# Splitting one group's output product around the next group's first layer in a fused attention and MLP kernel

## Chip, core and metric

The kernel runs on one core of one Trainium2 chip. The metric is device time in microseconds (us), the median of several runs. A core has five engines that work side by side, each through its own list of instructions in order: TensorE (PE: matmuls, with the weight loads in front of them), VectorE (DVE), ScalarE (ACT), GpSimd (POOL) and SyncE (SP, which here only issues DMAs). POOL and ACT issue some DMAs too. Matmul results go to PSUM, which the kernel treats as eight banks of 128 x 512 float32.

## What is computed

```
k_p, v_p = mean of k, v over 8 neighbouring positions       # q, k, v: (8, 8, 576, 64)
attn     = softmax(q @ k_p^T / sqrt(64)) @ v_p              # per batch and head
x        = attn as (4608 tokens, 512)
h        = x @ w_in                                         # w_in: (512, 2048)
out      = (h - tanh(h)) @ w_out                            # w_out: (2048, 512)
```

## The kernel before

**Groups.** The 4608 tokens are worked as nine groups of 512: groups 0 to 7 are the first 512 tokens of batches 0 to 7, group 8 is the eight remainders of 64. For each group there is a *first layer*: 16 tiles of 128 hidden rows x 512 tokens, four matmuls each, then a tanh on ACT and a subtract on DVE that writes g = h - tanh(h) as bf16 into `Gt`. Then comes the output product with w2 (`w_out`).

**Group 0** is special. Its first layer (lines 946 to 960) makes one tile at a time (`mlp_h`). Its output product is the plain one (`mlp_o`, line 586): four token blocks tb of 128, each a chain of 16 matmuls in one PSUM bank. The chains are done a quarter at a time in the order `W2_ORDER = (0, 8, 4, 12)`, so that a quarter of w2 (four of its sixteen row blocks) has to be there only when its turn comes. One *unit* below is four such matmuls, one tb and one quarter; there are 16. After a chain's last quarter ACT copies it to `O`, and after each second one SP stores two blocks.

**Groups 1 to 8** make the first layer in pairs (`h_pair`, line 616): tiles p and p + 8 into two neighbouring banks, one tanh and one subtract of 128 x 1024 for both. Pair 0 is computed in two halves of the tokens, since its second half needs the later x blocks. The eighth pair is made as two single tiles (`h_one`). The output product is done with seven products of half-size blocks instead of eight (`products`, line 689), for which DVE makes sums of `Gt` (`sum_p`, `sum_q`, `sum_d`) and the kernel once makes sums of w2's blocks b11, b12, b21, b22 (`w_sum`, line 647, into `w2s`; b12 itself is replaced by b22 - b12 at the end). Half of those sums is made on DVE, w2s 3 on POOL, and the negative of b22 (w2s 4) on ACT.

**Attention of the next batch** is laid between these. For batch 1 this falls into group 0's output product, in lines 961 to 1030, where the order is written out by hand by unit number u: POOL adds the raw keys together (`pool_k`, line 240; its last add, which makes `kd`, is DVE's here), ACT casts q to bf16 in three parts (`q1_cast` twice, then the last 64 tokens), PE turns keys and queries by matmuls with an identity (`k_transpose`, `q_pe_transpose`), DVE and ACT copy them out of PSUM (`KB`, `qT`), scores go through exp on ACT (`scores_wide`, `scores_ends`), DVE adds the values together and masks them into `VB` (`pool_v`, line 267), `av` (line 516) multiplies and DVE divides by the sums (a reciprocal and a multiply), and PE turns the five results of 128 tokens into xT (`x_pe_transpose`, copied by ACT), except the fifth, which belongs to group 8 and is turned by DMA. For the later batches queries, keys and x are turned by DMA transposes issued from SP, and `v_spread` places the values by three DMAs.

**PSUM banks** are given out by small counters: `Banks(5, 6, 7)` serves attention, banks 0, 1, 3, 4 hold the four output chains of group 0, and `h_pair` is told its first bank: (2, 0, 4, 6, 0, 2, 4) for group 1, (0, 2, 4, 6, 0, 2, 4) later.

**Queues.** Each engine follows the program's order; a tile framework adds the semaphores, and `after` adds a few waits by hand. w2 is loaded by POOL with a cast from float32 to float16: quarters 0 and 8 early (lines 812, 814), and inside `pool_k(1)` blocks 4 and 5, 6 and 7 after the first add and quarter 12 after the second (line 961, `mid`). SP's order through this part is: batch 1's queries and values (lines 943, 944), a transpose for group 8, batch 2's keys (line 963, held until blocks 6 and 7 of w2 have landed), values and queries, group 0's stores, then in group 1's loop the transposes of batch 2's keys and x end at pair 0, its queries at pairs 2, 3 and 4 (`c = p - 2`, each right behind ACT's cast `q_cast_part`), the three spreads, and batch 3's keys, values and queries. In group 1's products SP issues the transposes of batch 2's x, which group 2's first layer reads.

Of the kernel before, what the change touches and what calls it, by code (L numbers as in the profile page):

```python
# [20 lines left out]
R = 4  # L21
# [6 lines left out]
TG = 512  # L28
# [15 lines left out]
def kernel(  # L44
# [192 lines left out]
    def halves(n, b):  # L237
        return ((0, n),) if b < 2 else ((0, n // 2), (n // 2, n))

    def pool_k(b, eng, t0=0, t1=NT, mid=(), last=None, dep2=None):  # L240
        r = k_raw[b % 2].rearrange("p t (j d) -> p t j d", d=D)[:, t0:t1, :, :]
        if b not in kdups:
            kdups[b] = work.tile([128, NT, 2, D], BF16, name="kd", tag="kd", bufs=1)
        kd = kdups[b][:, t0:t1, :, :]
        n = t1 - t0
        for ta, tb in halves(n, b):
            eng.tensor_tensor(  # L247
                out=r[:, ta:tb, 0:4, :], in0=r[:, ta:tb, 0:4, :], in1=r[:, ta:tb, 4:8, :], op=ALU.add
            )
        for i, m in mid[0:2]:  # L250
            load_w2(i, m)
        second = eng.tensor_tensor(
            out=r[:, :, 0:2, :], in0=r[:, :, 0:2, :], in1=r[:, :, 2:4, :], op=ALU.add
        )
        if dep2 is not None:
            after([second], dep2)
        for i, m in mid[2:]:
            load_w2(i, m)
        kd_done = (last or eng).tensor_tensor(
            out=kd,  # L260
            in0=r[:, :, 0:1, :].to_broadcast([128, n, 2, D]),
            in1=r[:, :, 1:2, :].to_broadcast([128, n, 2, D]),
            op=ALU.add,
        )
        return kd_done

    def pool_v(b, eng):
        r = v_raw[b % 2].rearrange("p t (j d) -> p t j d", d=D)
        for ta, tb in halves(NT, b):
            eng.tensor_tensor(  # L270
                out=r[:, ta:tb, 0:4, :], in0=r[:, ta:tb, 0:4, :], in1=r[:, ta:tb, 4:8, :], op=ALU.add
            )
        eng.tensor_tensor(
            out=r[:, :, 0:2, :], in0=r[:, :, 0:2, :], in1=r[:, :, 2:4, :], op=ALU.add
        )
        if b < 2:
            eng.tensor_tensor(
                out=r[:, :, 0, :], in0=r[:, :, 0, :], in1=r[:, :, 1, :], op=ALU.add
            )
            v_main(VB[b % 2], r[:, :, 0:1, :], eng, 0, NM)  # L280
            return v_left(VB[b % 2], r[:, NM, 0:1, :], eng)
        if b < 4:
            eng.memset(VB[b % 2][0:G, 0:H, D:D1], float(POOL))
        vps[b] = work.tile([128, NT, D], BF16, name="vp", tag="vp", bufs=1)
        return eng.tensor_tensor(
            out=vps[b][:, :, :], in0=r[:, :, 0, :], in1=r[:, :, 1, :], op=ALU.add
        )

    vps = {}

# [5 lines left out]

    def v_main(vb, vs, eng, t0, t1):
        n = t1 - t0
        eng.tensor_tensor(
            out=vb[:, 2 * t0 : 2 * t1, 0:D].rearrange("p (t s) d -> p t s d", s=2),  # L300
            in0=vs[:, t0:t1, :, :].to_broadcast([128, n, 2, D]),
            in1=mask[:, 2 * t0 : 2 * t1, :]
            .rearrange("p (t s) o -> p t s o", s=2)
            .to_broadcast([128, n, 2, D]),
            op=ALU.mult,
        )
# [276 lines left out]

    o_tiles = {}

    def mlp_o(g, tb, qd, gts, pool=None, k0=0, k1=4):
        if qd == 0:
            p, tag = pool or (ps_o, "o_ps")
            o_tiles[tb] = p.tile([128, DM], FP32, name="o_ps", tag=tag)
        o_ps = o_tiles[tb]  # L590
        i0 = W2_ORDER[qd]
        for i in range(i0 + k0, i0 + k1):
            nc.tensor.matmul(  # L593
                o_ps[:, :],
                lhsT=gts[i][:, tb * 128 : (tb + 1) * 128],
                rhs=w2b[:, i, :],
                start=(i == 0),
                stop=(i == NHID - 1),
            )
        if qd == 3:  # L600
            nc.scalar.copy(out=O[:, tb, :], in_=o_ps[:, :])
            if tb % 2:
                store(g, tb - 1, tb + 1, nc.sync)
# [337 lines left out]
    ps_h.n = ps_o.n = 0  # L941
    nc.scalar.copy(out=q_bf[:QT, R, :, :], in_=t0[:QT, :, R, :])
    load_q(1, False)
    load_main(v_pairs, v_raw[1], 1, 0, NM)
    load_q_tail(1, q_raws[1], nc.scalar)
    for i in range(5):
        mlp_h_mms(0, i, 2, 4)
# [1 line left out]


    for i in range(5, NHID):
        mlp_h(0, i, gts, bank((0, 1, 2, 3, 4, 0, 1, 2, 3, 4, 2)[i - 5], [128, TG]))
        if i == 7:
            q_pe_tail(0)
        if i == 9:
            scores_tail(0)
        if i == 11:
            ps_a.n = 0
            av(0, 4, ps_any, True)
            x_dma_transpose(0, 2)  # L960
    kd1 = pool_k(1, nc.gpsimd, mid=((4, 2), (6, 2), (12, 4)), last=nc.vector)
    after([w_sum(w2s[:, 3, :, :], b21, b11, ALU.subtract, nc.gpsimd, k, k + 2) for k in (0, 2)], kd1)
    after(load_k(2), w2_dmas[3])
    load_v(2)

    def q1_cast(t, h):
        nc.scalar.copy(
            out=q_bf[:, 0:R, h : h + 4, :].rearrange("p j h d -> p h j d"),
            in_=t[:, h : h + 4, 0:R, :],
        )  # L970

    o_pools = [(ps_o, "o_ps"), (ps_o, "o_ps"), (ps_h, "hT_ps"), (ps_h, "hT_ps")]
    pend = []
    for u in range(16):
        qd, tb = u // 4, u % 4
        if u == 8:
            scores_wide(1, (3,))
            scores_ends(1)
        if qd == 2:
            for t2 in (2 * (tb % 2), 2 * (tb % 2) + 1):  # L980
                mlp_o(0, t2, qd, gts, o_pools[t2], tb // 2 * 2, tb // 2 * 2 + 2)
        else:
            mlp_o(0, tb, qd, gts, o_pools[tb])
        if u == 0:
            q1 = q_raws.pop(1)
            q1_cast(q1, 0)
        if u == 3:
            k_transpose(1, ps_any, (nc.vector.tensor_copy, nc.vector.tensor_copy))
        if u == 4:
            q_pe_transpose(1, (0, 1), "act")  # L990
            q1_cast(q1, 4)
            nc.scalar.copy(out=q_bf[:QT, R, :, :], in_=q1[:QT, :, R, :])
            load_q(2)
            w_sum(w2s[:, 1, :, :], b11, b12, ALU.add, k1=4)
            w_sum(w2s[:, 0, :, :], b11, b22, ALU.add, k1=4)
            w_sum(w2s[:, 2, :, :], b21, b22, ALU.add, k1=4)
            w_sum(b12, b22, b12, ALU.subtract, k1=4)
            v1_done = pool_v(1, nc.vector)
            after(
                [  # L1000
                    w_sum(w2s[:, 3, :, :], b21, b11, ALU.subtract, nc.gpsimd, k, k + 2)
                    for k in (4, 6)
                ],
                v1_done,
            )
            w_sum(w2s[:, 1, :, :], b11, b12, ALU.add, k0=4)
        if u in (5, 6):
            q_pe_transpose(1, (u - 3,), "act")
        if 5 <= u <= 7:
            scores_wide(1, (u - 5,))  # L1010
        if u == 6:
            q_pe_tail(1)
        if u in (9, 11):
            n = (u - 9) // 2
            nc.scalar.mul(
                out=w2s[:, 4, 4 * n : 4 * n + 4, :], in_=b22[:, 4 * n : 4 * n + 4, :], mul=-1.0
            )
        if 11 <= u <= 14:
            x_pe_transpose(1, *pend.pop(0))
        if 9 <= u <= 12:  # L1020
            pend.append((u - 9, av(1, u - 9, ps_any, False)))
        if u == 13:
            w_sum(w2s[:, 0, :, :], b11, b22, ALU.add, k0=4)
            sums = w_sum(w2s[:, 2, :, :], b21, b22, ALU.add, k0=4)
        if u == 15:
            ps_a.n = 0
            av(1, 4, ps_any, True)
    pool_k(2, nc.gpsimd, dep2=sums)
    pool_v(2, nc.gpsimd)
    w_sum(b12, b22, b12, ALU.subtract, k0=4)  # L1030

    for g in range(1, NG):
        nb = g + 1 if g + 1 < B else None
        nn = g + 2 if g + 2 < B else None
        for p in range(NP - 1):
            c = p if g > 1 else p - 2
            if nb is not None and 0 <= c < 3:
                q_cast_part(nb, c)
            h_pair(g, p, ((2, 0, 4, 6, 0, 2, 4) if g == 1 else (0, 2, 4, 6, 0, 2, 4))[p], p % 2)
            if 3 <= p < 6:  # L1040
                sum_p(2 * p - 6, 2 * p - 4)
            if nb is not None and p == 0:
                k_dma_transpose(nb)
            if g == 1 and p == 0:
                x_dma_transpose(1, 2)
            if g > 1 and p == 0:
                store(g - 1, 2, 4, nc.gpsimd)
                store(g - 1, 0, 2, nc.gpsimd)
            if nb is not None and p == 0:
                k_place(nb, nc.gpsimd.tensor_copy)  # L1050
            if nb is not None and 0 <= c < 3:
                q_dma_transpose(nb, c)
# [6 lines left out]
        h_one(g, NP - 1, 1, 0, 2)  # L1059
        h_one(g, NP - 1, 0, 1, 3)  # L1060
        sum_p(6, 8)
        sum_q(0, 4)
        sum_q(4, 8)
        if nb is not None:
            sum_d(0, 2)
            sum_d(2, 4)
        ps_a = Banks(2, 3, 4, 5, 0, 1)
        for u in range(14):
            n, half = u // 2, u % 2
            bk, lhs, rhs = products[n]  # L1070
# [57 lines left out]
```

The softmax here doesn't subtract the row's maximum and nothing guards it: scores larger than these inputs give would overflow.

## Time and profile before

| | us |
|---|---|
| median of three runs (lowest, highest) | 286.85 (286.12, 287.18) |
| the profiled execution | 289.25 |
| its span, first to last instruction | 287.5 |
| PE busy in it | 276.5 (96%) |
| DVE, ACT, POOL busy | 221.3, 158.0, 113.8 |
| granted TensorE clock | 1.00 |
| group 0's output product with batch 1's attention | 34.84 to 56.15 |
| group 1's first layer, its products | 56.15 to 71.64, 71.64 to 87.31 |
| group 2's first layer, its products | 87.31 to 101.30, 101.30 to 116.30 |

A line of the timeline reads: start in us from the span's start, length, engine, line of the kernel, operation, tile written <- tiles read, shapes, number of instructions merged, and in brackets the idle time of that engine just before, with what ended it. "PEld" is the weight load of PE, "SPq" a DMA issue on SP. A line of the chain of waits has start, length and what the chain went through. A line of the DMA issues has the tiles, the issuing queue, the number, the size of one in KB and the median us from issue to landing. A line of the table by stretch has the stretch, its length, the busy us of PE, PEld, DVE, ACT and POOL with the number of instructions, the granted clock, the DMA engines' share and GB/s.

### The profile page before, as it was taken

To read this page: it belongs to the slowest core of one execution; us is meant where nothing else is said; L and a number is where in the kernel's file an instruction comes from. 1 tells how busy PE (TensorE), PEld (TensorE's weight loads), DVE (VectorE), ACT (ScalarE), POOL (GpSimd) and SP (SyncE) were. 2 spreads that over 40 slices of the span, in tenths; PEclk is the share of its full clock that TensorE was granted. 3 is DMA by queue.
4 is the path that set the end of the run, shared out by engine and by line. 5 is a ranking of instruction groups with operands and counts; after the bars stand their busy time and mean duration, and the time that the engine had idled before them with its cause. 6 is when DMAs were issued, how large, how long until landed. Compare 5 with 4: busy or idle time off the path is not lost.

```text
span 287.5 us, 5465 instructions
## 1 busy us (share of the span) xinstructions
PE 276.5 (96%) x2156; PEld 179.7 (63%) x2156; DVE 221.3 (77%) x338; ACT 158.0 (55%) x212; POOL 113.8 (40%) x124
## 2 busy tenths in 40 slices
PE   7799989997999999999999999999999999999994
PEld 3364444643796479647964796479647964884583
DVE  6567878748985898589858985898589838945993
ACT  4637656757817681768176817681768146315510
POOL 8500650794089208920892089208930110000000
PEclk9999999999999999999999999999999999999999
DMA  7999999995997898689859965798560350002014
GB/s 242 229 213 264 308 123 187 328 275 107 295 233 113 222 339 202 85 215 350 191 102 222 355 160 100 227 335 177 101 186 0 51 179 0 2 40 109 0 36 112
DMA packets 67253, 50.41 MB, mean 175 GB/s; under 512 B 42652, under 2 KB 56476, under 8 KB 67228
## 3 DMA queue, kind: packets, MB, share of 16 engines
q1 hardware_dynamic: 57724, 36.04, 50.0%
q0 software_dynamic: 6784, 12.06, 19.9%
q10 hardware_dynamic: 2720, 1.97, 2.4%
q8 instruction: 17, 0.28, 0.4%
q14 instruction: 8, 0.07, 0.1%
HBM read 36.70 MB, written 9.44 MB: 160 GB/s over the span
## 4 chain that ended last, share of the span: by engine, by line
PE 84%; DMA 7%; DVE 3%; ACT 2%; issue 1%; SPq 1%; ACTq 0%
PE PS L665 34%; PE PS L608 34%; PE PS L564 5%; DMA q_raw<-in_q_dram 4%; PE PS L448 3%; PE PS L593 3%; DMA k_raw<-in_k_dram 3%; PE PS L422 3%; DVE Gt L622 2%; PE PS L374 1%; DVE P L630 1%; ACT TS L621 1%; PE PS L463 1%; ACT qT L132 0%; PE PS L844 0%
## 5 line engine op out<-in xcount | busy, mean ns | idle before, releaser
L608 PE MATMUL PS<-xT,w1b 128*128 128x512 bf16 (+1 forms) x504 | 98.1, 355 | 1.5 <-DVE Gt L622 1.5
L622 DVE TENSOR_TENSOR Gt<-PS,TS 128x1024 bf16<-128x1024 f32 x56 | 68.4, 1221 | 35.3 <-ACT TS L621 35.3
L608 PEld LDWEIGHTS <-w1b 128*128 128x128 f16 x576 | 56.3, 98 | 54.3 <-issue 1.8
L621 ACT ACTIVATE TS<-PS 128x1024 f32<-128x1024 f32 x56 | 57.3, 1024 | 29.3 <-PE PS L608 27.1
L709 POOL TENSOR_TENSOR m<-O,m 128x512 f32<-128x512 f32 x6 | 7.6, 1260 | 78.5 <-ACT m L707 78.5
L665 PE MATMUL PS<-w2s,Dg 128*128 128x256 f16 x256 | 30.2, 273 | 0.0
L247 POOL TENSOR_TENSOR k_raw<-k_raw 128x512 f32<-128x512 f32 (+2 forms) x13 | 21.4, 1665 | 18.7 <-DMA k_raw<-in_k_dram 18.7
L443 ACT ACTIVATE E<-PS 72x1024 bf16<-72x1024 f32 (+1 forms) x30 | 26.1, 930 | 4.2 <-PE PS L422 4.0
L665 PEld LDWEIGHTS <-Gt 128*128 128x128 bf16 x256 | 23.5, 98 | 6.8 <-issue 2.3
L665 PEld LDWEIGHTS <-P 128*128 128x128 bf16 x256 | 24.5, 98 | 3.0
L665 PEld LDWEIGHTS <-Dg 128*128 128x128 bf16 x256 | 24.6, 98 | 2.8
L630 DVE TENSOR_TENSOR P<-Gt 128x1024 bf16<-128x1024 bf16 x32 | 22.1, 689 | 0.6
L716 ACT COPY m<-PS 128x512 f32<-128x512 f32 x8 | 4.7, 586 | 29.5 <-PE PS L665 29.5
L640 DVE TENSOR_TENSOR Dg<-Gt 128x1024 bf16<-128x1024 bf16 x32 | 20.4, 683 | 0.0
L681 POOL DMA_DIRECT2D out_dram<-O x14 | 7.7, 552 | 31.7 <-DVE O L719 29.5
L270 POOL TENSOR_TENSOR v_raw<-v_raw 128x512 f32<-128x512 f32 (+1 forms) x12 | 18.2, 1535 | 0.0
L499 DVE TENSOR_TENSOR x_sb<-PS,rden 128x512 bf16<-128x512 f32 x24 | 16.6, 692 | 0.8
L665 PE MATMUL PS<-w2s,Gt 128*128 128x256 f16 x128 | 16.4, 273 | 0.0
L665 PE MATMUL PS<-w2b,P 128*128 128x256 f16 x128 | 16.3, 273 | 0.0
L665 PE MATMUL PS<-w2b,Gt 128*128 128x256 f16 x128 | 16.3, 272 | 0.0
L665 PE MATMUL PS<-w2s,Q 128*128 128x256 f16 x128 | 16.3, 272 | 0.0
L1090 ACT COPY O<-PS 128x512 f32<-128x512 f32 x7 | 4.1, 586 | 21.9 <-PE PS L665 21.9
(120 smaller groups left out, 401.8 us busy)
## 6 DMA issues: line engine op xcount, KB each, us to landing
k_raw<-in_k_dram SPq DMA_DIRECT2D x7, 1024.0 KB, 5.8
q_raw<-in_q_dram SPq DMA_DIRECT2D x7, 1024.0 KB, 10.7
v_raw<-in_v_dram SPq DMA_DIRECT2D x7, 1024.0 KB, 7.9
out_dram<-O POOLq DMA_DIRECT2D x14, 512.0 KB, 3.9
w1b<-in_moe_w_in_dram POOLq DMA_DIRECT2D x4, 512.0 KB, 15.6
w2b<-in_moe_w_out_dram POOLq DMA_DIRECT2D x3, 512.0 KB, 25.3
out_dram<-O SPq DMA_DIRECT2D x2, 512.0 KB, 9.1
k_raw<-in_k_dram SPq DMA_DIRECT2D x7, 128.0 KB, 5.9
```

What stands on the lines that cost most here:

```text
L247: eng.tensor_tensor(out=r[:, ta:tb, 0:4, :], in0=r[:, ta:tb, 0:4, :], in1=r[:, ta:tb, 4:8, :], op=ALU.add)
L270: eng.tensor_tensor(out=r[:, ta:tb, 0:4, :], in0=r[:, ta:tb, 0:4, :], in1=r[:, ta:tb, 4:8, :], op=ALU.add)
L422: nc.tensor.matmul(dst, lhsT=kv[a * D : (a + 1) * D, m, :], rhs=rhs, start=True, stop=True,)
L443: nc.scalar.activation(out=e, in_=ps, func=ACT.Exp, scale=SCALE)
L499: nc.vector.tensor_tensor(out=x_sb[:, :, :, :], in0=ps[:, :, :, 0:D], in1=rden[:, :, :, :].to_broadcast([128, 2, 4, D]), op=ALU.mult,)
L564: nc.tensor.matmul(h_tiles[i][:, :], lhsT=w1b[:, fb, i * 128 : (i + 1) * 128], rhs=xT[g][:, :, fb, :], start=(fb == 0), stop=(fb == NFB - 1),)
L608: nc.tensor.matmul(dst[:, t0 * 128 : t1 * 128], lhsT=w1b[:, fb, i * 128 : (i + 1) * 128], rhs=x[:, t0:t1, fb, :], start=(fb == 0), stop=(f ...
L621: nc.scalar.activation(out=t2, in_=PS[:, b0 : b0 + 2, :], func=ACT.Tanh)
L622: nc.vector.tensor_sub(out=Gt[:, p, :, :], in0=PS[:, b0 : b0 + 2, :], in1=t2)
L630: nc.vector.tensor_tensor(out=P[:, a:b, :], in0=Gt[:, a:b, 0, :], in1=Gt[:, a:b, 1, :], op=ALU.add)
L640: return nc.vector.tensor_tensor(out=Dg[:, a:b, :, :], in0=Gt[:, a:b, :, 0:HT], in1=Gt[:, a:b, :, HT:TG], op=ALU.subtract,)
L665: nc.tensor.matmul(part(g, bk, tt), lhsT=lhs(k, slice(tt * 128, (tt + 1) * 128)), rhs=rhs[:, k, :], start=(first and k == 0 and (tt == 0 o ...
```

## The change

Four things are moved, and the hand-written loop over u becomes a straight list.

1. Group 0's 16 units are no longer done in a row. Ten of them (quarters 0 and 8 of all four blocks, quarter 4 of blocks 0 and 1) stay among batch 1's attention; the other six are a function, `rest_of_group_0`, which is called in group 1's loop ahead of pair 4, with four of DVE's sums and the last b12 sum behind it. The chains use banks 1, 2, 3, 0, and group 1's pairs the banks (6, 4, 6, 4, 6, 4, 2).
2. POOL issues w2's last two quarters as two whole loads behind the key adds and two of its w2 sums, instead of three loads between the adds. Batch 2's key load waits for quarter 4, which is now one load.
3. Batch 1's values are loaded in two halves and pooled on DVE in three parts (`pool_v1`): the leftover rows early, each half later.
4. In group 1, batch 2's query casts and transposes, key transpose, spreads and batch 3's loads move from pairs 2, 3, 4 (the key transpose: 0) to pairs 4, 5, 6 (4).

All five AV blocks of batch 1 now use two neighbouring banks at once, and all three casts of q stand ahead of the query turns on ACT.

```diff
+    def pool_v1(ta, tb):
+        r = v_raw[1].rearrange("p t (j d) -> p t j d", d=D)
+        for n in (4, 2, 1):
+            nc.vector.tensor_tensor(
+                out=r[:, ta:tb, 0:n, :],
+                in0=r[:, ta:tb, 0:n, :],
+                in1=r[:, ta:tb, n : 2 * n, :],
+                op=ALU.add,
+            )
+        if ta == NM:
+            return v_left(VB[1], r[:, NM, 0:1, :], nc.vector)
+        return v_main(VB[1], r[:, :, 0:1, :], nc.vector, ta, tb)
...
-            o_tiles[tb] = p.tile([128, DM], FP32, name="o_ps", tag=tag)
+            o_tiles[tb] = bank((1, 2, 3, 0)[tb], [128, DM])
...
-    load_main(v_pairs, v_raw[1], 1, 0, NM)
+    load_main(v_pairs, v_raw[1], 1, 0, 2)
+    load_main(v_pairs, v_raw[1], 1, 2, 4)
...
-        mlp_h(0, i, gts, bank((0, 1, 2, 3, 4, 0, 1, 2, 3, 4, 2)[i - 5], [128, TG]))
+        mlp_h(0, i, gts, bank(i % 5, [128, TG]))
...
-    kd1 = pool_k(1, nc.gpsimd, mid=((4, 2), (6, 2), (12, 4)), last=nc.vector)
-    after([w_sum(w2s[:, 3, :, :], b21, b11, ALU.subtract, nc.gpsimd, k, k + 2) for k in (0, 2)], kd1)
-    after(load_k(2), w2_dmas[3])
-    load_v(2)
...
+    ps_a = Banks(4, 5, 6, 7)
+    q1 = q_raws.pop(1)
+    kd1 = pool_k(1, nc.gpsimd, last=nc.vector)
+    after([w_sum(w2s[:, 3, :, :], b21, b11, ALU.subtract, nc.gpsimd, k, k + 2) for k in (0, 2)], kd1)
+    load_w2(4, 4)
+    load_w2(12, 4)
+    w_sum(w2s[:, 1, :, :], b11, b12, ALU.add, k1=4)
+    pool_v1(NM, NT)
+    mlp_o(0, 0, 0, gts)
+    q1_cast(0)
+    q1_cast(4)
+    nc.scalar.copy(out=q_bf[:QT, R, :, :], in_=q1[:QT, :, R, :])
+    mlp_o(0, 1, 0, gts)
+    mlp_o(0, 2, 0, gts)
+    k_transpose(1, ps_any, (nc.vector.tensor_copy, nc.vector.tensor_copy))
+    w_sum(w2s[:, 0, :, :], b11, b22, ALU.add, k1=4)
+    w_sum(w2s[:, 2, :, :], b21, b22, ALU.add, k1=4)
+    mlp_o(0, 3, 0, gts)
+    q_pe_transpose(1, (0, 1), "act")
+    mlp_o(0, 0, 1, gts)
+    scores_wide(1, (0,))
+    q_pe_transpose(1, (2,), "act")
+    pool_v1(0, 2)
+    mlp_o(0, 1, 1, gts)
+    scores_wide(1, (1,))
+    q_pe_transpose(1, (3,), "act")
+    q_pe_tail(1)
+    w_sum(b12, b22, b12, ALU.subtract, k1=4)
+    v1_done = pool_v1(2, 4)
+    mlp_o(0, 2, 1, gts)
+    scores_wide(1, (2, 3))
+    scores_ends(1)
+    mlp_o(0, 3, 1, gts)
+    ps_a.n = 0
+    av(1, 0, ps_any, True)
+    av(1, 1, ps_any, True)
+    mlp_o(0, 0, 2, gts)
+    turn1(0)
+    turn1(1)
+    av(1, 2, ps_any, True)
+    mlp_o(0, 1, 2, gts)
+    av(1, 3, ps_any, True)
+    after(load_k(2), w2_dmas[2])
+    load_v(2)
+    load_q(2)
+    av(1, 4, ps_any, True)
+    turn1(2)
+    turn1(3)
...
+    for n in range(2):
+        nc.scalar.mul(out=w2s[:, 4, 4 * n : 4 * n + 4, :], in_=b22[:, 4 * n : 4 * n + 4, :], mul=-1.0)
+    after(
+        [w_sum(w2s[:, 3, :, :], b21, b11, ALU.subtract, nc.gpsimd, k, k + 2) for k in (4, 6)],
+        v1_done,
+    )
+    w_sum(w2s[:, 1, :, :], b11, b12, ALU.add, k0=4)
+    w_sum(w2s[:, 0, :, :], b11, b22, ALU.add, k0=4)
+    sums = w_sum(w2s[:, 2, :, :], b21, b22, ALU.add, k0=4)
+    x_dma_transpose(1, 2)
     pool_k(2, nc.gpsimd, dep2=sums)
     pool_v(2, nc.gpsimd)
-    w_sum(b12, b22, b12, ALU.subtract, k0=4)
+
+    def rest_of_group_0():
+        for qd, tb in ((2, 2), (2, 3), (3, 0), (3, 1), (3, 2), (3, 3)):
+            mlp_o(0, tb, qd, gts)
+        sum_p(2, 4)
+        sum_q(0, 4)
+        sum_d(0, 2)
+        sum_d(2, 4)
+        w_sum(b12, b22, b12, ALU.subtract, k0=4)
...
-            c = p if g > 1 else p - 2
+            c = p if g > 1 else p - 4
+            if g == 1 and p == 4:
+                rest_of_group_0()
             if nb is not None and 0 <= c < 3:
                 q_cast_part(nb, c)
-            h_pair(g, p, ((2, 0, 4, 6, 0, 2, 4) if g == 1 else (0, 2, 4, 6, 0, 2, 4))[p], p % 2)
+            h_pair(g, p, ((6, 4, 6, 4, 6, 4, 2) if g == 1 else (0, 2, 4, 6, 0, 2, 4))[p], p % 2)
...
-            if nb is not None and p == 0:
+            if nb is not None and c == 0:
                 k_dma_transpose(nb)
-            if g == 1 and p == 0:
-                x_dma_transpose(1, 2)
...
-        ps_a = Banks(2, 3, 4, 5, 0, 1)
+        ps_a = Banks(*((4, 5, 2, 3, 0, 1) if g == 1 else (2, 3, 4, 5, 0, 1)))
```

## Prediction

> **What bounds it now.** I read the busy table by stretch first, then the chain that ended last, then the timelines of PE, ACT, DVE and SP from 34 to 90 us. The clock is 1.00 in every stretch, so busy PE time can be compared. Stretches (columns: length, then busy us of PE, PEld, DVE, ACT, POOL):
>
> ```profile
> 56.15:71.64 15.49, 14.00 (x76) 7.03 (x74) 10.63 (x12) 9.71 (x11) 11.72 (x12) 1.00 0.92 203
> 71.64:87.31 15.67, 15.17 (x169) 12.77 (x168) 14.80 (x25) 7.14 (x10) 7.22 (x5) 1.00 1.06 261
> 87.31:101.30 13.99, 13.99 (x76) 7.19 (x74) 9.93 (x11) 10.52 (x12) 7.99 (x11) 1.00 0.73 161
> 101.30:116.30 15.00, 15.00 (x171) 12.68 (x169) 14.00 (x24) 6.59 (x9) 7.38 (x5) 1.00 0.88 253
> 34.84:56.15 21.31, 20.04 (x152) 10.65 (x151) 16.05 (x34) 14.33 (x25) 8.97 (x8) 1.00 1.24 216
> ```
>
> Group 2, rows three and four, is PE end to end: 13.99 us of first layer, 15.00 of products. The change sits in the others: group 0's output product with batch 1's attention (**O**, last row, 21.31), group 1's first layer (**H**, first row, 15.49) and its products (**P**, second row, 15.67). H and P are 1.50 and 0.67 longer than group 2's. In O, 64 output matmuls are 64/16 x 3.45 = 13.8 (sixteen ran from 34.84 to 38.29) and the attention's small ones about 5.85 (41 turns of 0.056, the query tail 0.1, scores 1.7, AV 30 x 0.059), so 1.6 to 1.7 is waiting. All that can be won here is about 3.8 us. The chain and the timelines say why H waits:
>
> ```profile
> 50.29 12.59 DMA q_raw<-in_q_dram
> ...
> 63.91 1.02 ACT TS L621
> ```
>
> ```profile
> 58.16 1.02 ACT L621 ACTIVATE TS<-PS 128x1024 f32<-128x1024 f32 x1 [1.57 <-PE PS L608]
> ...
> 59.21 1.23 DVE L622 TENSOR_TENSOR Gt<-PS,TS 128x1024 bf16<-128x1024 f32 x1 [0.59 <-ACT TS L621]
> ...
> 62.95 1.04 ACT L184 CAST q_bf<-q_raw 128x1024 bf16<-128x1024 f32 x1 [2.05 <-DMA q_raw<-in_q_dram]
> ...
> 69.91 1.89 PE L608 MATMUL PS<-xT,w1b 128*128 128x512 bf16 x8 [1.49 <-DVE Gt L622]
> ```
>
> ACT stands before batch 2's query cast until the load lands at 62.9; tanh, subtract and PE follow late. One pair costs PE 13.83/8 = 1.73, ACT 1.02, DVE 1.23. The last thing to see is SP's queue, whose chain ends just in time:
>
> ```profile
> 71.28 0.58 SPq L138 DMA_DIRECT2D k_raw<-in_k_dram  x1
> ...
> 81.68 4.12 SPq L527 DMA_TRANSPOSE xT<-x_sb  x2
> ```
>
> ```profile
> q_raw<-in_q_dram SPq DMA_DIRECT2D x1, 1024.0 KB, 11.9
> ```
>
> Batch 3's loads start at 71.28; its queries (issued 73.82) land 11.9 later, at 85.7, which is 14.4 after the first issue. Batch 2's two x transposes, issued behind them on the same queue, land at 86.95 and 87.86, though their inputs were ready before 84: they waited for the loads. Group 2's first layer starts at 87.31 and needs the second at 87.31 + 0.86. The slack is 0.3 us.
>
> **The change, in order of time (us of the profiled execution).**
>
> *Start of O.* POOL's second key add no longer stands behind two DMA issues: it ends at 34.14 + 1.56 = 35.7 instead of 37.1. DVE's last group-0 subtract ends at 36.36, so kd (0.82) ends at 37.2, 0.8 earlier. PE does three units (four matmuls, 0.864 each) to 37.43, turns the keys, one unit to 38.6, and waits as before for the query cast (38.34 + 1.04 = 39.4), whose load I leave where it was. ACT now makes all three casts first (38.34 to 40.9), so qT 0 is copied at 41.4, not 40.5. On DVE a w2 sum (1.13, as the first beside POOL's sum now) and the leftover values (0.43 + 0.29 + 0.22 + 0.42 with gaps 1.5) go ahead of the KB copies, which end at 40.9, not 39.7. The first scores start at 41.45; PE waits 0.7. From there ACT paces it: last exp at 46.5 (47.0 before).
>
> *Values in halves.* Per half: 0.70 + 0.43 + 0.29 + 0.44, 1.95 with gaps. DVE: KB 40.9, two w2 sums 42.3, half one 44.25, b12 sum 44.95, half two 46.9. The whole load had landed by 44.2 before, so DVE sets this. The first AV matmuls run at 46.6 to 46.9, a microsecond before the 47.91 of now. This edit gains 1.0.
>
> *AV and turns.* But only ten of sixteen units are left to fill PE here, and AV blocks follow each other through DVE: reciprocal and multiply take 0.94 a block, 0.6 after its matmuls. Ends of the multiplies: 48.3, 49.24, 51.1 (after turn 1), 52.3, 53.24. PE waits about 0.7 before turn 1 and 0.85 before turn 2, whose banks AV 3 holds. Group 1's first pair writes banks 6 and 7, which AV 4 holds: it starts at 53.3. Six units (5.18) are still owed then, so this is like 58.5 against 56.15 now.
>
> *w2's last quarters.* Their issues move behind POOL's add, kd and two POOL sums (2.26): to 39.6 and 40.3 from 34.1, 34.8 and 37.05. The rows they move away from:
>
> ```profile
> w2b<-in_moe_w_out_dram POOLq DMA_DIRECT2D x2, 256.0 KB, 11.8
> w2b<-in_moe_w_out_dram POOLq DMA_DIRECT2D x1, 512.0 KB, 13.1
> xT_last<-x_end SPq DMA_TRANSPOSE x1, 11.5
> ```
>
> Ends: the store row's 3.9 for 512 KB gives 43.5; 13.1 gives 52.7. The w2 packets that started around 38 each took about 5 us, beside the transpose that took 11.5 and lagging value packets. I take 12.3 less 5.2: landed at 46.7, needed by PE at 47.45; no cost. The upper end costs 5.2. The last quarter then lands near 50 to 52, before its users at 54.8 (ACT) and 63 (PE). Batch 2's loads hang on the third quarter, 47.1 before, so they don't move.
>
> The Trainium skill, "DMA: Bandwidth & Descriptors", Anatomy of one DMA, gives such a DMA 2.0 us plus bytes over 436 GB/s; for 1 MB read that is an estimate of 4.4 us, against rows of 11.3 to 13.1 here. By the page alone the quarter lands near 44.7, by the longest row at 52.7.
>
> *Four pairs on two pairs of banks.* The output tiles keep banks 0 to 3, so pairs 0 to 3 alternate between 6,7 and 4,5; pair 2 waits for pair 0's subtract. Also ahead of tanh 0 on ACT are the turns' copies (to 53.9) and two w2 negations (1.06 each, to 55.9). Pair 0 ends on PE at 55.1, its tanh at 56.9, subtract at 58.1; pair 2 starts at 58.2 where PE was free at 56.8. That wait of 1.4 comes once; pair 3 ends at 61.7. The six units then run to 66.8, ACT and DVE catch up in them, and pairs 4 to 7 end H at 73.75. Now: 71.64. **+2.1.** The wait for batch 2's queries is gone (their cast comes at 67.5, the load lands at 62.9): that is H's 1.50, already in this sum. DVE's sums that move ahead of P can give back up to P's 0.67.
>
> *SP's queue.* Query casts move from pairs 2, 3, 4 to pairs 4, 5, 6. ACT reaches the first only behind the fourth O copy (67.5); the others follow tanh 4 and 5, the last ending at 72.15 (67.28 now). Behind it on SP stand a transpose (1.2) and three spreads (2.7): batch 3's loads are issued at 76.2, 2.4 after H's end, where now it is 0.36 before. From first issue to queries landed the other groups show 12.6, 13.2, 13.0 and 14.0, this one 14.4; from there to the first x transpose 1.25. Taking 13.4 + 1.3: group 2 starts at 90.9. PE alone would get there at 73.75 + 15.0 to 15.67 = 88.8 to 89.4. So SP's queue ends last. 90.9 - 87.31 = **+3.6**; with 12.6 to 14.4, 2.8 to 4.6. From group 2 on the order is the old one, period 28.8, PE bound, so the shift stays to the end. POOL's keys and values of batch 2 were ready at 61.65 and 67.2 and are not late; the spread lands about 78, AV of batch 2 starts about 80.
>
> **Sum.** The profiled execution took 289.25 us with a span of 287.5; the median of the runs shown is 286.85, 2.4 below. I put the difference on the median: 286.85 + 3.6 = **290.5**.
>
> **Rivals.**
> 1. *Only PE's own waits count*: batch 3's loads run at DMA speed with no engine lagging, x is in time. For: 13 of the 16 DMA engines' shares of that query load had landed by 83.84, and the last came at 85.70. Against: four more groups take at least 12.6. Then 73.75 + 15.0 to 15.67: +1.5 to +2.1, 288.6.
> 2. *The third w2 quarter late*: PE stands at 47.45 until up to 52.7, and all behind it. For: the rows of 11.3 to 13.1. Against: the stuck packets. PE's order lets nothing pass the waiting matmul, so 2 to 5 us come on top of the forecast: 292.5 to 295.5.
> 3. *Faster*: the waits in O and H together cost only what O's cost now (1.65), since H's wait for the queries is gone. Its place is tanh 0 and pair 2's bank wait; H would end at 34.84 + 19.65 + 13.85 + 1.65 = 70.0, and with products of 15.0 group 2 starts at 85.0: -2.3, 284.5. It decides from the point where H ends before 70.9 and batch 3's loads go out before 71.2. Against: pair 2's wait is arithmetic, 1.02 + 1.23 against 1.73, and SP's casts are three pairs from the end.
> 4. *Nothing*: H's gain and O's loss cancel and the loads are just in time, or the split changes who waits only: 286.9.
>
> **Chances.** Forecast 0.50 (289.3 to 291.8); rival 1 0.17, of which 0.02 within 0.5%; rival 2 0.12; rival 3 0.08; rival 4 0.13. Slower by over 0.5% (1.4 us, about what a measurement of this kernel can tell from no change): 0.50 + 0.15 + 0.12 = 0.77; within: 0.15; faster: 0.08. The range leaves out rival 3 and most of rival 2: 286.6 to 292.8.
>
> **What would show it.** AV 0 before 47.2; group 1's first matmul near 53.3; PE waiting for a Gt subtract before pair 2, near 57 to 58; the six late units unbroken around 62 to 67; H's end near 73.7; batch 3's first load near 76; PE waiting for xT at group 2's start, near 89 to 91. I am wrong if the first layer of group 1 ends before 72, if the loads go out before 73, or if PE stands in front of w2b near 47.

## The result and the profile after

| | before | changed |
|---|---|---|
| median of four runs (lowest, highest), us | 286.49 (285.71, 287.18) | 294.49 (294.15, 297.21) |
| ratio, 95% interval | | 1.0297 [1.0239, 1.0355] |

The changed kernel is slower, as forecast, but by 8.0 us and not by 3.6. The stretches of its profiled execution (297.21 us, span 295.3) are, in the columns of the table by stretch: group 0's ten units with attention (O), group 1's first layer up to the six late units, those units, the rest of the layer (these three are H), the products (P), and group 2's first layer.

```profile
35.33:54.10 18.77, 15.04 (x129) 8.33 (x128) 16.39 (x33) 9.99 (x18) 7.86 (x8) 1.00 0.84 209
54.10:63.09 8.99, 7.24 (x41) 3.99 (x41) 7.09 (x6) 5.52 (x7) 7.62 (x6) 1.00 0.71 197
63.09:68.27 5.18, 5.18 (x25) 2.35 (x24) 4.68 (x5) 2.78 (x4) 4.30 (x4) 1.00 0.04 18
68.27:75.18 6.91, 6.91 (x34) 3.18 (x33) 5.59 (x8) 6.42 (x8) 0.97 (x3) 1.00 0.93 245
75.18:93.41 18.23, 14.98 (x168) 12.49 (x167) 12.64 (x21) 8.21 (x11) 10.63 (x7) 0.99 0.91 228
93.41:108.90 15.49, 15.49 (x74) 7.97 (x75) 9.45 (x10) 8.98 (x10) 4.52 (x9) 0.90 0.79 191
```

Length less the first busy number is PE's idle time: 3.73 in O, 1.75 in the first piece of H, none beside the late units or after them, 3.25 in P. Group 2's first layer has no idle time and is still 1.5 longer than the 13.99 of before: its granted clock is 0.90. The timeline of PE names the waits:

```profile
42.28 0.38 PE L377 MATMUL PS<-qT,KB 128*128 128x512 bf16 x1 [1.74 <-DVE KB L325]
...
59.48 3.61 PE L610 MATMUL PS<-xT,w1b 128*128 128x512 bf16 x16 [1.75 <-DVE Gt L624]
...
93.41 0.82 PE L610 MATMUL PS<-xT,w1b 128*128 128x256 bf16 x3 [3.25 <-DMA xT<-x_sb]
```

The chain of waits goes through the same places: DVE's three w2 sums and a subtract ahead of pair 2, then PE, then the DMA transpose of x.

```profile
54.04 4.25 DVE w2s L650 x3
58.29 1.14 DVE Gt L624
59.48 3.61 PE PS L610 x16
63.09 5.18 PE PS L595 x24
68.27 6.91 PE PS L610 x32
...
84.37 8.99 DMA xT<-x_sb
93.41 15.49 PE PS L610 x72
```

Batch 2's query cast no longer waits for its load, but it comes late, between the last O copy and tanh 4 (ACT), and SP's queue follows it: batch 3's first load is issued at 77.58 (71.28 before), and x waits in the queue behind these loads.

```profile
68.79 1.05 ACT L184 CAST q_bf<-q_raw 128x1024 bf16<-128x1024 f32 x1
```

```profile
77.58 0.58 SPq L138 DMA_DIRECT2D k_raw<-in_k_dram  x1
...
84.37 7.16 SPq L530 DMA_TRANSPOSE xT<-x_sb  x2
```

Batch 3's queries, issued at 80.12, land 11.5 later, at 91.61; group 2 starts 1.8 after that.

### The profile page after: what moved, and what is told of

Read it like the earlier page. It is cut to its first block, busy times and chain, and to the rows that moved or that the text cites. A ratio compares the mean times of both kernels' runs of the same rounds, so it can differ in the third digit from the quotient of the medians.

```text
span 295.3 us, 5461 instructions
## 1 busy us (share of the span) xinstructions
PE 277.6 (94%) x2156; PEld 180.5 (61%) x2156; DVE 225.3 (76%) x337; ACT 158.1 (54%) x212; POOL 113.8 (39%) x123
## 4 chain that ended last, share of the span: by engine, by line
PE 83%; DVE 7%; DMA 6%; issue 1%; ACT 1%; SPq 0%; DVEq 0%
PE PS L610 37%; PE PS L667 32%; PE PS L567 5%; DMA xT<-x_sb 3%; DMA k_raw<-in_k_dram 3%; PE PS L425 3%; PE PS L451 2%; DVE w2s L650 2%; PE PS L595 2%; DVE v_raw L282 2%; PE PS L466 1%; DVE x_sb L502 0%; DVE VB L302 0%; PE PS L846 0%; DVE Gt L624 0%
## 5 line engine op out<-in xcount | busy, mean ns | idle before, releaser
L610 PE MATMUL PS<-xT,w1b 128*128 128x512 bf16 (+1 forms) x504 | 99.8, 360 | 5.2 <-DMA xT<-x_sb 3.2
L610 PEld LDWEIGHTS <-w1b 128*128 128x128 f16 x576 | 57.0, 99 | 59.1 <-DMA xT<-x_sb 3.5
L623 ACT ACTIVATE TS<-PS 128x1024 f32<-128x1024 f32 x56 | 57.3, 1024 | 34.0 <-PE PS L610 32.8
L632 DVE TENSOR_TENSOR P<-Gt 128x1024 bf16<-128x1024 bf16 x32 | 23.3, 730 | 0.6
L502 DVE TENSOR_TENSOR x_sb<-PS,rden 128x512 bf16<-128x512 f32 x28 | 19.4, 691 | 1.0
L719 DVE TENSOR_TENSOR m<-m,m 128x512 f32<-128x512 f32 x8 | 12.0, 1498 | 5.1 <-ACT m L718 5.1
## 6 DMA issues: line engine op xcount, KB each, us to landing
q_raw<-in_q_dram SPq DMA_DIRECT2D x7, 1024.0 KB, 11.5
w2b<-in_moe_w_out_dram POOLq DMA_DIRECT2D x4, 512.0 KB, 15.9
```

Source lines behind the costliest of these rows:

```text
L502: nc.vector.tensor_tensor(out=x_sb[:, :, :, :], in0=ps[:, :, :, 0:D], in1=rden[:, :, :, :].to_broadcast([128, 2, 4, D]), op=ALU.mult,)
L610: nc.tensor.matmul(dst[:, t0 * 128 : t1 * 128], lhsT=w1b[:, fb, i * 128 : (i + 1) * 128], rhs=x[:, t0:t1, fb, :], start=(fb == 0), stop=(f ...
L623: nc.scalar.activation(out=t2, in_=PS[:, b0 : b0 + 2, :], func=ACT.Tanh)
L632: nc.vector.tensor_tensor(out=P[:, a:b, :], in0=Gt[:, a:b, 0, :], in1=Gt[:, a:b, 1, :], op=ALU.add)
L719: nc.vector.tensor_tensor(out=m4, in0=m4, in1=m45, op=ALU.subtract)
```

## Experiments

The theory was the forecast's: SP's queue ends last (late casts, so late loads, so late x). Against it stood that PE's own waits in O and H make the loss, and, after the profile, that the clock makes a part of it. "On after" and "on before" say which kernel a diff changes. Ratios are of medians, against the kernel before on the same chip.

### Both kernels once more

```diff
(no edit: before and after as they are)
```

> The kernel before, unchanged, profiled once more. Theory: the execution that the prediction was made from was not a typical one; its first layer of group 1 waited 1.5 us for batch 2's queries, which the typical execution does not. A second profile shows a first layer of 13.8 to 14.2 us and 63.5 to 65 us from the start of group 0's output product to the products of group 2, where the first showed 15.5 and 66.3. Rival: the wait is in every execution, and the second profile shows 15 to 15.5 and 66 again.

> The changed kernel, unchanged, on the same chip. 294 to 294.5 by both theories; its profile shows 39.7 us from the start of group 0's output product to group 1's products, 15.5 to 17 from batch 3's first load to the first x transpose, and a half clock only if PE stood for over 3 us before group 2.

c_before: 285.61 us, ratio 0.9988 [0.9969, 1.0007]; c_after: 295.03 us, 1.0312 [1.0271, 1.0352]. Their profiled executions took 284.98 and 293.54 us. The table by stretch of c_before (O, H, P, group 2's first layer):

```profile
33.25:54.03 20.78, 19.62 (x153) 10.77 (x151) 16.59 (x34) 14.44 (x25) 11.00 (x11) 1.00 1.14 284
54.03:67.86 13.83, 13.83 (x75) 7.05 (x73) 10.46 (x12) 10.16 (x12) 9.54 (x10) 1.00 0.81 173
67.86:82.95 15.09, 15.09 (x169) 12.76 (x168) 14.22 (x25) 6.65 (x10) 7.22 (x5) 1.00 1.05 271
82.95:96.79 13.84, 13.84 (x75) 7.02 (x73) 9.78 (x11) 10.52 (x12) 8.00 (x11) 1.00 0.74 162
```

and of c_after (O, H with the late units, P, group 2's first layer):

```profile
33.53:52.31 18.78, 15.21 (x129) 8.26 (x127) 16.40 (x33) 10.00 (x18) 8.79 (x8) 1.00 0.96 249
52.31:72.62 20.31, 19.17 (x96) 9.39 (x96) 16.41 (x17) 14.72 (x19) 12.11 (x12) 1.00 0.63 169
72.62:91.09 18.47, 15.16 (x169) 12.65 (x168) 12.82 (x21) 8.22 (x11) 10.65 (x7) 1.00 0.89 226
91.09:104.94 13.85, 13.85 (x73) 7.06 (x74) 9.29 (x10) 8.99 (x10) 4.53 (x8) 1.00 0.82 188
```

In c_before H and P are PE end to end: there is no wait for batch 2's queries at all. Its cast follows tanh with no idle time in front of it, at 58.68 and not at 62.95:

```profile
58.68 1.04 ACT L184 CAST q_bf<-q_raw 128x1024 bf16<-128x1024 f32 x1
```

The key load that leads these queries on SP is held until blocks 6 and 7 of w2 have landed. That load took 9.7 from issue to landing in c_before and 12.3 in the execution of the prediction; the keys went out 9.74 after O's start in c_before and 12.30 after it in the execution of the prediction, and the queries landed at 56.67 and 62.88. The first key load on SP, in c_before and in the execution of the prediction:

```profile
42.99 0.38 SPq L138 DMA_DIRECT2D k_raw<-in_k_dram  x1
```

```profile
47.14 0.38 SPq L138 DMA_DIRECT2D k_raw<-in_k_dram  x1
```

The keys' delay of 2.56 is more than the 2.05 that ACT stood before the cast, so the 1.50 of H belongs to that one execution. The run with values in halves below, whose w2 loads are those of the kernel before, does not have the wait either. What delayed the keys is likely w2's packets, though no run tests it: 25 of those started near 38 took 4.6 to 5.8 us each in the execution of the prediction, and none as much as 3 us between 33 and 50 in c_before, nor in either profile of the changed kernel. That O's 0.5 and P's 0.6 have the same origin is likely, not shown.

### Batch 3's keys and values ahead of batch 2's transposes (on after)

```diff
     x_dma_transpose(1, 2)
+    load_k(3)
+    load_v(3)
     pool_k(2, nc.gpsimd, dep2=sums)
...
                 if nn is not None:
-                    load_k(nn)
-                    load_v(nn)
+                    if g > 1:
+                        load_k(nn)
+                        load_v(nn)
                     load_q(nn)
```

> The changed kernel with one thing moved: batch 3's key and value loads are issued on SP right behind the group-8 transpose of batch 1 (near 57 us), not behind the three spreads (77.6 us); its query load stays. Queue theory: group 2 waits 3.2 us only because its x transposes stand behind 3.4 MB of loads that SP issued too late. With 2.25 MB of them gone early, group 2's first layer follows the products directly (about 90.2 us in the profile instead of 93.4), the clock has no idle time to fall in, and the time is 289.6 to 291.3. Rival (x is late for a reason of its own: its issue, the AV blocks, the stores): group 2 starts near 93 and the time stays at 294.

290.81 us, 1.0190 [1.0175, 1.0206]. H, P and group 2's first layer:

```profile
52.11:73.10 20.99, 19.17 (x97) 9.37 (x96) 17.26 (x17) 14.71 (x19) 13.51 (x12) 1.00 1.09 282
73.10:88.09 14.99, 14.99 (x170) 12.74 (x169) 12.34 (x21) 6.58 (x9) 7.22 (x5) 1.00 0.49 124
88.09:101.92 13.83, 13.83 (x74) 7.05 (x72) 9.77 (x11) 10.51 (x12) 7.97 (x11) 1.00 0.66 159
```

P is PE alone again: the wait for x is the queue's, and taking two of three loads out of its way removes it. O and H keep their loss. So about 1.2% of the 3.1% is the queue and 1.9% is O and H: both theories are right, each for its part. O and H are 5.2 us longer here than in c_before; 4.2 of this is idle time of PE, and the rest is recorded as busy time, why is open.

### Only the late casts (on before)

```diff
-            c = p if g > 1 else p - 2
+            c = p if g > 1 else p - 4
...
-            if nb is not None and p == 0:
+            if nb is not None and c == 0:
                 k_dma_transpose(nb)
...
-            if nb is not None and p == 0:
+            if nb is not None and c == 0:
                 k_place(nb, nc.gpsimd.tensor_copy)
```

> The kernel before with the change's fourth part alone: batch 2's query casts and transposes and its key transpose at pairs 4, 5, 6, so that batch 3's loads go out later. Queue theory: group 1's first layer no longer waits for batch 2's queries and ends 1.5 earlier (70.1 us), but batch 3's loads go out near 72.5 instead of 71.3 and group 2 waits for its x transposes until 88 to 89: 287.2 to 288.5, and 1.7 more if the clock falls. Rival (the queue doesn't matter, PE's own waits count): the wait for the queries is gone and nothing takes its place: 285.0.

288.30 us, 1.0115 [1.0083, 1.0146]. O and H are those of c_before (20.77 and 13.84), and P alone grows, from 15.09 to 17.99, by the same DMA in the chain. This part is the queue alone, and with the 1.0190 of the run above it makes up about the whole.

```profile
68.04:86.03 17.99, 15.35 (x170) 12.69 (x168) 14.88 (x25) 8.41 (x12) 9.94 (x7) 1.00 0.94 228
```

```profile
77.68 8.30 DMA xT<-x_sb
85.98 0.05 issue
86.03 4.17 PE PS L608 x26
```

### Late casts with early loads (on before)

```diff
(the edit of only the late casts, and)
                 k_dma_transpose(nb)
+                if g == 1:
+                    load_k(3)
...
             if nb is not None and c == 2:
+                if g == 1:
+                    load_v(3)
                 v_spread(nb)
                 if nn is not None:
-                    load_k(nn)
-                    load_v(nn)
+                    if g > 1:
+                        load_k(nn)
+                        load_v(nn)
```

> The kernel before with batch 2's query casts at pairs 4, 5, 6 (as in the run with that part alone), and with batch 3's keys issued on SP right behind batch 2's key transpose and its values ahead of the spreads, so that only its queries are left for the old place. Queue theory: that part alone gave back in group 2's wait (18.0 us from the products' start to group 2, not 15.0) just what it won in the first layer (13.8 instead of 15.5); with the loads out of the way of the x transposes both are had: products to group 2 in 15.0 to 15.3, 2.5 to 3 us less than before, 282.5 to 283.3. Rival (batch 2's query transposes now stand behind the key load, and the scores of batch 2 wait as long): 285 to 286.

286.08 us, 1.0018 [0.9995, 1.0042]. P comes back from 17.99 to 15.86, not all the way to the 15.09 of c_before. The gain over the kernel before that was expected is a miss: it was to be H's wait for the queries, and both kernels have an H of 13.83.

### PE kept busy while it waits for x (on after)

```diff
             nc.scalar.copy(out=O[:, 0:2, 0:HD], in_=chain(g, C1))
+        if g == 1:
+            warm_pe(14, b0=3)
```

Fourteen matmuls of zeros stand at the end of group 1's products; they add nothing to the output.

> The changed kernel with 14 matmuls of zeros (3.0 us at full clock) on PE between group 1's last product and group 2's first layer, into a bank that nothing uses there; the output is the same. Clock theory: the half clock from 93.1 to 96.5 us in the profile follows from the 3.25 us of idle PE; without the idle time group 2's first layer takes 13.9 us instead of 15.5, so the profiled execution gains 1.5 to 1.7, and the median gains as much if its runs drop too, less if only some do. Rival (the layer is long for another reason, such as the second x transpose): it stays at 15.5 and the time at 294.5.

295.55 us, 1.0355 [1.0340, 1.0370]. P and group 2's first layer:

```profile
73.64:93.08 19.44, 18.13 (x182) 14.00 (x182) 12.82 (x21) 8.21 (x11) 11.59 (x8) 1.00 0.93 215
93.08:106.92 13.84, 13.84 (x72) 7.07 (x73) 9.29 (x10) 8.98 (x10) 3.58 (x8) 1.00 0.74 192
```

The layer runs at full clock in 13.84, where the profile after had 15.49 at 0.90, and all four executions had a mean clock of 0.998 or more. But c_after shows a layer of 13.85 without this edit, so the half clock is in some executions only: of its four, 293.54 and 294.57 us had a mean clock of 0.999 and 0.998, 295.49 and 295.67 had 0.994 and 0.993. That the edit keeps the clock up agrees with this, and is not proved by it. The time does not fall: P is 1.0 longer here than in c_after, waiting for x. The loads go out 2.54 after H's end, as in c_after, and the queries land 14 us after the first of them, as there; the extra time lies behind that landing, 2.9 until group 2 starts and not 2.05. Why is not settled.

### DVE's and ACT's w2 work behind the late units (on after)

```diff
-    for n in range(2):
-        nc.scalar.mul(out=w2s[:, 4, 4 * n : 4 * n + 4, :], in_=b22[:, 4 * n : 4 * n + 4, :], mul=-1.0)
...
-    w_sum(w2s[:, 1, :, :], b11, b12, ALU.add, k0=4)
-    w_sum(w2s[:, 0, :, :], b11, b22, ALU.add, k0=4)
-    sums = w_sum(w2s[:, 2, :, :], b21, b22, ALU.add, k0=4)
...
-    pool_k(2, nc.gpsimd, dep2=sums)
+    pool_k(2, nc.gpsimd)
...
     def rest_of_group_0():
+        for n in range(2):
+            nc.scalar.mul(out=w2s[:, 4, 4 * n : 4 * n + 4, :], in_=b22[:, 4 * n : 4 * n + 4, :], mul=-1.0)
...
         sum_d(2, 4)
+        w_sum(w2s[:, 1, :, :], b11, b12, ALU.add, k0=4)
+        w_sum(w2s[:, 0, :, :], b11, b22, ALU.add, k0=4)
+        w_sum(w2s[:, 2, :, :], b21, b22, ALU.add, k0=4)
         w_sum(b12, b22, b12, ALU.subtract, k0=4)
```

> The changed kernel with the three later w2 sums on DVE (4.3 us beside POOL) and the two negations on ACT moved from ahead of group 1's first pair into the stretch with the six late units; the wait of POOL's second key add on those sums is left out with them. Theory: they delay the first subtract by 1.2 us and so pair 2, the whole of group 1's first layer, the query casts and SP's loads; without them all of that comes 1.1 to 1.3 earlier, and the time is 293.3. Rival (two pairs of banks set the pace whatever else stands on DVE and ACT, or the moved sums come back as a wait in the products): no gain, 294 to 295.

295.04 us, 1.0338 [1.0320, 1.0356]: no gain. H is 19.88, 0.4 less than in c_after and 1.2 less than in the profile after, but P is longer (18.78): the loads follow H's end by 2.54 as in c_after, and from the first load to group 2's start it takes 16.2 and not 15.9. In this execution the half clock made group 2's layer 16.64, and all four executions had a mean clock under 0.995. DVE's three sums took 1.89 here, away from POOL's adds, against 4.33 in the profile after, which is the second line:

```profile
66.75 1.89 DVE L650 TENSOR_TENSOR w2s<-w2b 128x1024 f16<-128x1024 f16 x3
```

```profile
53.96 4.33 DVE L650 TENSOR_TENSOR w2s<-w2b 128x1024 f16<-128x1024 f16 x3
```

The same edit with early loads:

```diff
(this edit, and that of batch 3's keys and values ahead)
```

> The changed kernel with batch 3's keys and values issued early and the three later w2 sums and the negations moved into the stretch of the six late units: two of the experiments together. Queue theory: alone, the later sums won 1.1 us in the first layer and lost it again in the wait for batch 3's loads; with that wait gone they count, and 39.8 us become 38.7: 289.5 to 290.0, against 290.8. Rival (the sums come back as a wait in group 1's products): 290.8.

289.80 us, 1.0125 [1.0089, 1.0160]. With the queue out of the way the sums count: O and H take 38.66 together against 39.77 with early loads alone, and P stays at 14.99. The saving shows once the other wait is gone; how much of it the queue and how much the clock had hidden in the run before is not separated.

### Two more units in front, with early loads (on after)

```diff
     turn1(0)
+    mlp_o(0, 1, 2, gts)
     turn1(1)
     av(1, 2, ps_any, True)
-    mlp_o(0, 1, 2, gts)
+    mlp_o(0, 2, 2, gts)
     av(1, 3, ps_any, True)
...
     av(1, 4, ps_any, True)
+    mlp_o(0, 3, 2, gts)
     turn1(2)
...
-        for qd, tb in ((2, 2), (2, 3), (3, 0), (3, 1), (3, 2), (3, 3)):
+        for qd, tb in ((3, 0), (3, 1), (3, 2), (3, 3)):
```

> The changed kernel with batch 3's keys and values issued early, and two of the six late units (quarter 4 of blocks 2 and 3) moved back among batch 1's AV blocks and turns, so that twelve units stand there and four come late. Theory: PE's waits between AV blocks and turns (about 1.4 us) are filled: 38.4 us from the start of the output product to group 1's products, 289.4. Rival (with two units fewer above them, DVE's four sums and the last w2 sum before pair 4's subtract stick out, as they did with no late units): 39.2 to 39.8, no gain.

289.79 us, 1.0136 [1.0092, 1.0180]. O is 19.03 with two units more in it (18.78 without), so 1.5 of their 1.73 fill PE's waits, and O and H take 38.15 together. P is 1.1 longer than with early loads alone (16.10), because PE waits for the transposes of batch 2's queries. SP had issued them by 71.53, no earlier than with early loads alone (71.67), while H ended 1.3 earlier:

```profile
73.86 0.62 PE L425 MATMUL PS<-qT,KB 64*72 64x512 bf16 x4 [1.04 <-DMA qT<-q_bf]
```


### All units in front, with early loads (on after)

```diff
(the edit of two more units, all sixteen placed between the AV blocks and turns, and early loads)
-            h_pair(g, p, ((6, 4, 6, 4, 6, 4, 2) if g == 1 else (0, 2, 4, 6, 0, 2, 4))[p], p % 2)
+            h_pair(g, p, ((2, 0, 4, 6, 0, 2, 4) if g == 1 else (0, 2, 4, 6, 0, 2, 4))[p], p % 2)
```

> The changed kernel with batch 3's keys and values issued early (as in the first experiment), and with the split undone: the six late units go back among batch 1's AV blocks and turns, and group 1's pairs use four pairs of banks again. Theory: the AV blocks' waits (0.34, 0.24, 0.44, 0.74, 0.23 us on PE) are filled and pair 2's wait (1.75) goes, so from the start of group 0's output product to the start of group 1's products it is 36 to 37 us, not 39.8: 287.0 to 288.0, against 290.8 with the split. Rival (the late units cost nothing where they were, DVE and ACT set the pace): 39 to 40 us, 290 to 291.

291.56 us, 1.0213 [1.0195, 1.0231]: a miss. DVE's block of four group sums and the b12 sum, which stands ahead of pair 4's subtract, was covered by the late units; without them PE waits for the subtract. DVE and then PE:

```profile
64.70 1.96 DVE L632 TENSOR_TENSOR P<-Gt 128x1024 bf16<-128x1024 bf16 x2
66.58 0.68 DVE L637 TENSOR_TENSOR Q<-Gt 128x1024 bf16<-128x1024 bf16 x1
67.18 1.28 DVE L642 TENSOR_TENSOR Dg<-Gt 128x1024 bf16<-128x1024 bf16 x2
68.39 0.68 DVE L650 TENSOR_TENSOR w2b<-w2b 128x1024 f16<-128x1024 f16 x1
68.99 2.35 DVE L624 TENSOR_TENSOR Gt<-PS,TS 128x1024 bf16<-128x1024 f32 x2
```

```profile
70.25 2.62 PE L610 MATMUL PS<-xT,w1b 128*128 128x512 bf16 x8 [2.61 <-DVE Gt L624]
```

So this run does not tell what the split alone costs; the DVE order is part of it.

### The two small edits alone (on before)

```diff
-    kd1 = pool_k(1, nc.gpsimd, mid=((4, 2), (6, 2), (12, 4)), last=nc.vector)
+    kd1 = pool_k(1, nc.gpsimd, last=nc.vector)
     after([w_sum(w2s[:, 3, :, :], b21, b11, ALU.subtract, nc.gpsimd, k, k + 2) for k in (0, 2)], kd1)
-    after(load_k(2), w2_dmas[3])
+    load_w2(4, 4)
+    load_w2(12, 4)
+    after(load_k(2), w2_dmas[2])
```

> The kernel before with the change's second part alone: w2's last two quarters as two whole loads behind the key adds and two of POOL's w2 sums. Theory: the earlier issue only fed packets that stood until the lagging value load was through, so nothing is lost; the third quarter lands near 46 in either, and the time is 285.5 to 286.0 (no change). Rival (a load issued 5 us later lands 5 us later): PE stands before the third quarter near 46, +2 to +5.

w2 late: 286.26 us, 1.0026 [1.0012, 1.0041]. PE does not stand in front of w2b; O is 21.05 and H 14.22, so a few tenths are lost.

```diff
-    load_main(v_pairs, v_raw[1], 1, 0, NM)
+    load_main(v_pairs, v_raw[1], 1, 0, 2)
+    load_main(v_pairs, v_raw[1], 1, 2, 4)
...
-            v1_done = pool_v(1, nc.vector)
+            pool_v1(NM, NT)
+            pool_v1(0, 2)
+            v1_done = pool_v1(2, 4)
```

> The kernel before with the change's third part alone: batch 1's values loaded in two halves and pooled in three parts, all at the old place in DVE's order. Theory (the prediction's): AV starts about a microsecond sooner, since DVE no longer waits 1.57 us for the whole load; the time falls by 0 to 1 us, less if batch 2's queries hold the first layer anyway: 284.8 to 285.5. Rival (twelve smaller operations take longer than five): the same or slower by up to 0.5.

Values in halves: 286.12 us, 1.0014 [0.9995, 1.0032], no change where a gain of up to 1 us was expected; the first AV matmul starts 12.89 after O's start, as in c_before. None of the ten edited kernels was faster than the kernel before.

## Why the prediction was wrong in size

Its own terms, against what two profiled executions of the same call measured (us; "before" of the prediction is the execution that it was made from):

| stretch | before, in the prediction | changed, predicted | c_before | c_after |
|---|---|---|---|---|
| O and the six units | 21.31 | 23.64 | 20.78 | 23.96 |
| H without them | 15.49 | 15.27 | 13.83 | 15.13 |
| P, to group 2's start | 15.67 | 17.15 | 15.09 | 18.47 |
| sum | 52.47 | 56.06 | 49.70 | 57.56 |
| difference | | +3.6 | | +7.9 |

The forecast for the changed kernel was 1.5 short; what it was subtracted from was 2.8 too long.

1. **The step that failed most: "I put the difference on the median."** The profiled execution took 2.4 more than the median, and I took the stretches of the one for those of the other. Much of the excess lay in the stretch that the change rewrites: against c_before's execution, which is 4.3 shorter, it began O 1.6 later and then took 2.8 longer, O 0.5, H 1.7, P 0.6. "H's 1.50, already in this sum" credits the change with a wait that c_before does not have; "all that can be won here is about 3.8 us" is some 1.2 there. Put on the execution's own time the same difference gives 289.25 + 3.6 = 292.85. That this is near the 293.54 of c_after's profiled execution is in part luck, since O began 1.3 earlier there.
2. **SP's queue: right in kind, short by 1.2.** The loads went out 2.54 after H's end in c_after (2.4 forecast). From first load to group 2's start it took 15.93 there, and 15.83 in the profile after, against 13.4 + 1.3: the queries landed 13.9 and 14.0 after the first issue, inside the 12.6 to 14.4 that I had, and group 2 started 2.05 and 1.80 after them, not 1.3. The runs of the early loads and of the late casts alone show that this queue sets P. Rival 1 falls with them.
3. **O and H: nearly as forecast.** O took 18.78 (18.46), the first AV came 12.04 after O's start (11.8 to 12.1), H with the late units 20.31 (20.45), the units ran unbroken. PE's wait before the first scores was 1.08 in c_after and 1.74 in the profile after, not 0.7: it ended with the KB copies, and the leftover values ahead of them on DVE took 3.27 in both and not 1.5. The microsecond of the values in halves is not shown to be theirs, since alone they moved AV by nothing. Inside H pair 2 waited 1.14 in c_after and 1.75 in the profile after (1.4 forecast). For DVE's three sums in front of pair 0's subtract the prediction has no term; they took 3.55 and 4.33, with POOL's key adds beside them. In c_after they ended together with tanh 0 (55.72 and 55.78) and cost nothing; in the profile after they ended 0.7 behind it (58.29 and 57.57). A row for their length stood in the trace of before: the w2 sum at 57.27, beside such an add, took 1.35.
4. **w2's later quarters: right.** They were issued at 40.44 and 41.22 and landed at 45.97 and 49.24 (46.7 and 50 to 52 forecast), and PE waited for neither. Rival 2 is refuted; the measured 294.49 lies in the range that it named, but for other reasons. The estimate put the longest rows of before down to lagging packets, and that holds for a part of them only: in c_before, without such packets, the three loads of these quarters still took 9.3, 9.7 and 10.9, issued earlier against O's start than here. So 46.7 came out near the mark partly by luck. For the Trainium skill's "DMA: Bandwidth & Descriptors", Anatomy of one DMA, the estimate was 4.4 us for such a quarter (from the issue at 39.6 that is 44.0, and not the 44.7 of the prediction); the two took 5.5 and 8.0, so the page's figure is a floor here.
5. **Rivals 3 and 4** needed H to end before 70.9 or the losses to cancel; H ended at 75.18, with O begun only 0.5 later than in the prediction. Rival 3 took the same wait of 1.50 for a gain that could be had.
6. **Not foreseen: the clock.** The half clock in some executions made group 2's layer 1.5 longer in the profile after. What it is worth in the median is not shown: the run with busy PE lost about as much to a later x, and in the first measurement one execution with a mean clock of 0.992 took 294.54, no more than one with 0.998 (294.59).

## What to carry to other kernels

Before a wait is subtracted from a time, profile the kernel a second time: a wait that one execution has and the next has not may be the part of the time by which that execution stands above the median. Follow each queue to its end, not only the engine: a cast moved two pairs later moved three loads, and the transposes behind them set the next group. And price a DVE operation by the row where POOL was working beside it, if it will be there again.

## What the runs showed of the hardware

- **Clock.** In the profile after the granted clock was 0.50 for 3.41 us from 93.07, 2.9 into PE's wait of 3.25; in the run with all units in front, 0.50 for 3.41 us from 71.26, 1.0 after a wait of 2.61 had ended; with the sums behind the late units, 0.50 for 6.83 us from 89.53, 2.1 into a wait of 3.24. c_after idled 3.32 and kept 1.00. The Trainium skill, "TensorE: Matmul & The Clock Gate", Part 1: The HAM clock gate, has the clock halved after an idle window of about 3.4 us, and lets that window run free of the kernel. The lengths of the drops agree, one window or two, and like waits with and without a drop are no contradiction. But none of these waits was as long as a window, so the drops themselves do not follow from the page. If the 3.41 us just before each drop is the window that counted, PE stood idle in 2.9, 2.4 and 2.1 us of it: an estimate from the times above.
- **DVE beside POOL.** Three float16 sums of 128 x 1024 took 1.89 and 1.88 in the two runs where POOL stood idle beside them, and 3.55, 4.33, 4.41 and 4.58 in c_after, the profile after and the runs with early loads and with busy PE, where its adds ran beside them (for 3.2 of the 4.33). Other causes were not separated: single sums that ran partly beside such adds took 0.69 in the trace of before and 0.68 in c_before, no more than elsewhere.
- **Queue behind loads.** In the five profiles where PE waited for x behind a batch's loads, group 2 started 1.3 to 2.9 after the queries, the last large load, had landed; with two of the three loads issued 20 us earlier, P had no wait at all.
- **Slow packets.** The 4.6 to 5.8 us packets of w2 came in one of fourteen profiled executions; in the others none between 33 and 50 took over 3.1 us. What makes them is open.
